# Recurrent-memory attention block with gradients: second buffers for exponentials and turned O in the forward stage, and the work around them rearranged

## The chip, the cores and the metric

The kernel runs on one core of one Trainium2 chip. The metric is the device time of one execution in microseconds (us). The engines of the core are called as in the profile: PE is TensorE (the matrix unit; PEld is its loading of weights), DVE is VectorE, ACT is ScalarE, POOL is GpSimd and SP is SyncE, which here only issues transfers (DMAs). "SPq" in a row is the transfer queue that SP feeds.

## The reference

A transformer block with conditioning, forward and backward: the kernel returns the output and the gradients of eleven inputs. The forward part is:

```
mod = (silu(c) @ w_mod)  split into  sa, ca, ga, sb, cb, gb      # 6 rows of 512
h = layernorm(x) * (1 + ca) + sa
x = x + ga * A(h)
h = layernorm(x) * (1 + cb) + sb
x = x + gb * ((sigmoid(h @ w_gate) * (h @ w_up)) @ w_down)       # w_gate: 512 x 1792

A(h):  mem = mem0                               # 8 rows of 512
  for s in range(64):                           # 2048 tokens, 32 a segment
    h_s = concat(mem, h[32 tokens of s])        # 40 rows
    q, k, v = h_s Wq, h_s Wk, h_s Wv            # 32 heads of 128
    p = softmax(mask(q k^T / sqrt(128)))        # causal; the 8 memory columns are always seen
    o = (p v) Wo
    mem = o[:8];  out_s = o[8:]
```

The eight memory rows that leave a segment enter the next one, so the 64 segments are one chain in the forward part and again, the other way, in the backward part. x has 2048 rows of 512.

## The kernel before

The work is a row of stages, each a method of one class: setup and the first LayerNorm, the forward attention (`phase2`, about 45 to 957 us of the profiled span), the gated block (`phase3`, to about 1600 us), the backward attention and the last products. The change lies in `phase2` and in what it loads and computes ahead for `phase3`.

`phase2` runs a loop over the 64 segments `s`; `s4 = s % 4` is the place of a segment in a row tile, since four segments of 32 tokens fill the 128 rows in which LayerNorm works. The 32 heads are laid out in `G = 11` groups of three. One segment goes like this:

- `proj` and `v_chunk`: q, k and v of the segment from its turned rows `hT` (products into `pass_ps`, copies into the row buffers `RA` and `Vst`, two each). `rows_out` stores the q and k rows on SP's queue (L604, L605). `turns` turns q and k by heads into `XT`.
- `st_exp`: the scores, three pieces into `st_ps`, and ScalarE's exponentials into `ET` (L869). There is one `ET`.
- SP transposes `Vst` into `VTr` (L1007) and `ET` into `Pst` (L1015), both by DMA; there is one buffer of each. They, O and turned O are kept in memory for the backward part. `norm`, put off to the beginning of the next segment, lets GpSimd scale `Pst` by the reciprocal sums `rden` (L1091) and SP store `VTr` and `Pst` (L1093, L1094).
- `den` and `pv`: sums and p v from `ET` into `or_ps` (L873 is the matmul of the sums). `ost` scales them into `Ost`, one buffer (VectorE for the first and the third piece at L917, ScalarE for the second); TensorE turns `Ost` in `tps` (L885) and the copies (L63 on VectorE, L61 on ScalarE, which are the two lines of the common helper `evac`) make `OT`, turned O. There is one `OT`. SP stores `Ost` to OSR (L1044) and `OT` (L1061).
- `outproj`: the product with Wo into `at_ps` (`pair_mm`, L223, 64 small matmuls). `split_pair` (L227 to L233) splits the result into `at_hi` (ScalarE, L230) and `at_lo` (VectorE, L232), `sum_pair` adds the two through TensorE (`at_ft`, L242), and ScalarE copies the first eight columns into the next segment's `hT`: that closes the chain. `store_rows` sends the other rows to AOA (L345).

Four other kinds of work are laid between these steps:

- LayerNorm for the row tiles ahead: `p1(j, k)` runs step `k` of tile `j` (0 load at L396, 1 statistics at L400, 2 scale, 3 shift, 4 turn). With `P1_AHEAD = 2` the statistics come in segments with `s4 = 2`, the scale in `s4 = 3`, the shift in `s4 = 0`, the turn in `s4 = 1`.
- The eight last rows of the four segments of a tile are projected together for q and k (`b_pieces`): products into `RB`, stored at L609 and L612 in `s4 = 1` and 2, turned into the tail columns `b_cols` of k and q (pool `p2bt`, two buffers). `tails_in` (GpSimd copies) puts the eight columns of the next segment into `XT`; `v_tails` (GpSimd DMAs) does this for v.
- `TailRows` collects the eight last columns of `OT` of each of the four segments (`collect`) in one tile, and turns them into rows with products laid between the steps of the next four segments (`chunk`, `split`).
- The first row tile of the gated block is begun in the last segments (`first_tile_steps`): loads of x, of attention output rows (AOA) and of the gradient rows, broadcasts of the conditioning rows 2 to 5, then residual, LayerNorm and turn.

Program order on each engine is the order in which the code calls these (`self.pin(i0)` holds it as written); the tile pools add the waits that a buffer's reuse needs. All transfers named above but GpSimd's go through SP's one queue in its program order. The beginning of `phase3` is touched as far as SP loads its row tiles behind this stage: VectorE's GLU chain starts at L1206, TensorE turns w_down at L1182.

Of the kernel before, what the change touches and what calls it, by code (L numbers as in the profile page):

```python
# [40 lines left out]
class K:  # L41
# [336 lines left out]
    def phase1_setup(self, ctx, psum_tile_fn):  # L378
# [55 lines left out]

        return p1_tile
# [9 lines left out]
    def phase2(self):  # L445
# [15 lines left out]
        with ExitStack() as ctx:  # L461
# [29 lines left out]
            ET = ptiles("ET", 1)[0]  # L491
            Vsts = ptiles("Vst", 2)
            Ost = ptiles("Ost", 1)[0]
            OT = ptiles("OT", 1)[0]
# [55 lines left out]
            btp = ctx.enter_context(tc.tile_pool(name="p2bt", bufs=2))  # L550
# [67 lines left out]
            def b_pieces(t):  # L618
# [14 lines left out]
                def turn_b(x):  # L633
                    bt[x] = btp.tile([128, 8, 128], BF16, name="b_cols" + x)
# [4 lines left out]
                    def f():  # L639
                        for hf in range(2):  # L640
# [79 lines left out]
            def first_tile_steps():  # L720
# [5 lines left out]
                bc = {2: self.sa_bc[:], 4: self.ca1_bc[:]}  # L726
                x1, sm = self.first_x1, self.first_st

                def load():
# [3 lines left out]
                    nc.sync.dma_start(dout, io["grad_out"].rearrange("o s d -> (o s) d")[0:128, :])  # L733
                    nc.gpsimd.memset(sm[:, 10:11], -0.5)

                def load_mod():
                    for i, x in ((3, "k"), (5, "q")):
                        bc[i] = f32(btails[NT - 2][x][:].rearrange("p i x -> p (i x)"))
                    for i in (2, 5, 4, 3):
                        nc.sync.dma_start(bc[i], self.MODROW[:, i * D:(i + 1) * D].rearrange("o d -> (o d)").partition_broadcast(128))  # L740

                def gates():
                    nc.vector.tensor_tensor(db, dout, bc[5], op=ALU.mult)
# [21 lines left out]
                def mods():  # L765
                    for i in (2, 5, 3):
                        nc.gpsimd.tensor_copy(self.bcs[i], bc[i])
                    nc.gpsimd.tensor_scalar_add(self.bcs[4], bc[4], 1.0)
# [8 lines left out]
                return load, load_mod, gates, add, stats, scale, rows, mods, turn  # L777
# [11 lines left out]
            tail = TailRows(self, sb2, psp, psp, 1, "ao", rows_b, (8, 16, 8), ptag="p")  # L789
# [34 lines left out]
            for s in range(NS):  # L824
# [13 lines left out]
                QT, KT, Vst = XT["q"], XT["k"], Vsts[s % 2]  # L838
# [164 lines left out]
                if 0 < s < NS - 1:  # L1003
                    v_chunk(s, 2)
                    v_tails(s + 1)
                if s < NS - 1:
# [39 lines left out]
                evac_turned()  # L1046
                for k in {0: (1, 2), 1: (3,)}.get(s, ()):
                    p1(P1_AHEAD, k)
                if s4 in (0, 2) and s > 0:
                    p1(s // nseg_t + P1_AHEAD + (s4 > 0), {2: 1, 0: 3}[s4])  # L1050
                if NS - 4 <= s < NS - 1:
                    first_tile[s - NS + 4]()
                elif s == NS - 1:
                    first_tile[6]()
                if s + 1 < NS:
                    tails_in("kq", s + 1)
                parts = self.split_pair(sb2, at_ps, "at")
                if s4 == 3:
                    p1(s // nseg_t + P1_AHEAD + 1, 2)
                tail.collect(s4, [OT])  # L1060
# [22 lines left out]
                if s4 == 0:  # L1083
                    tail.chunk()
                tail.split()
# [1213 lines left out]
class TailRows:  # L2299
# [3 lines left out]
    def __init__(self, k, pool, psp, psb, n, name, dram_b, npieces=4, home=None, ptag="b"):  # L2303
        self.k, self.pool, self.psp, self.psb, self.n, self.name = k, pool, psp, psb, n, name
        self.dram_b, self.npieces, self.home, self.ptag = dram_b, npieces, home, ptag
        self.cur = None
# [3 lines left out]
    def collect(self, s4, tiles):  # L2310
        nc, cfg = self.k.nc, self.k.cfg
        if self.cur is None:
            self.cur = [self.pool.tile([128, 33, 32], BF16, name=f"{self.name}_tail{i}") for i in range(self.n)]
# [145 lines left out]
```

## Time and profile before

| | us |
|---|---|
| three runs | 2984.21, 2986.32, 2985.37; median 2985.37 |
| profiled execution | 2986.66, of which span 2984.7 |
| forward stage, about | 45 to 957 |
| PE busy over the span | 2916.5 |
| PE busy in 45 to 250, 250 to 500, 500 to 750, 750 to 957 us | 197.23, 247.67, 245.22, 197.33 |
| mean granted clock of TensorE | 0.996 |

The page of the profile gives busy times, the chain and the groups of instructions over the whole span; the views that the trace answers give the same for a stretch. A row of the waits names the waiting engine, the tile that it wanted to write or read, what it waited for, the sum in us, how many waits and the mean of one. A row of the timeline gives the start in us, the duration, the engine, the line, the operation with its tiles, and in brackets the idle time before it with what ended it. A row of a tile gives the fewest, median and most ns of an instruction and where the first and the last began. The shares of busy time over the whole span mix stages with different limits; those of a stretch do not.

### The profile page before, as it was taken

The page shows a single profiled execution, that of the slowest core. Times are in us where ns is not written, and L with a number is a line of the kernel's source. Part 1 is how long each engine was busy: PE and PEld are TensorE (multiplying, and loading weights), DVE is VectorE, ACT ScalarE, POOL GpSimd, SP SyncE. Part 2 cuts the span into 40 slices and gives each one's busy share as a digit, 9 for nine tenths or more (in the row PEclk, how much of TensorE's full clock was granted, in tenths as well). Part 3 has the DMA queues.
Part 4 walks back from the last instruction along what each step waited for, and adds up shares of the span by engine and source line. Part 5 has one row for each costly group of instructions (what it writes and reads, how often), then busy time and mean ns, then how long its engine had stood idle before and what let it go on. Part 6 is the DMA issues. An engine that isn't in the chain of part 4 may idle for free.

```text
span 2984.7 us, 105439 instructions
## 1 busy us (share of the span) xinstructions
PE 2916.5 (98%) x43816; PEld 1817.4 (61%) x43816; DVE 1622.8 (54%) x3680; ACT 1348.8 (45%) x3244; POOL 1235.0 (41%) x2485
## 2 busy tenths in 40 slices
PE   6999999999998999999999999999999999999999
PEld 3666666666665544445677777777777754445555
DVE  5665666665554788833365566656566632850011
ACT  3666666666665533312355555555555520110011
POOL 2555555554555222221244444444444422762111
PEclk9999999999999999999999999999999999999999
DMA  9988999888889899998699999999999997886565
GB/s 309 225 215 220 215 214 225 215 218 207 217 218 270 210 229 233 229 282 280 202 249 234 266 249 250 255 253 250 252 250 252 247 280 249 253 262 190 160 216 171
DMA packets 837922, 703.01 MB, mean 236 GB/s; under 512 B 537682, under 2 KB 709890, under 8 KB 836548
## 3 DMA queue, kind: packets, MB, share of 16 engines
q1 hardware_dynamic: 711828, 485.29, 66.2%
q0 software_dynamic: 54512, 148.63, 15.7%
q10 hardware_dynamic: 71104, 62.34, 6.5%
q8 instruction: 345, 5.65, 0.8%
q14 instruction: 133, 1.09, 0.1%
HBM read 294.99 MB, written 276.35 MB: 191 GB/s over the span
## 4 chain that ended last, share of the span: by engine, by line
PE 69%; DMA 2%; ACT 1%; DVE 1%; issue 1%; SPq 0%; POOL 0%; DVEq 0%; ACTq 0%; POOLq 0%
PE gps L2240 14%; PE dh_ps L215 8%; PE pass_ps L257 7%; PE g_ps L1863 5%; PE gps5o L2255 4%; PE dhq_ps L223 4%; PE mm L1344 3%; PE dh_tps L215 3%; PE gps L1523 3%; PE mm L1304 2%; PE mm L1319 2%; PE tps L1780 2%; PE mm L1277 1%; PE mm L1273 1%; PE gps L1422 1%; PE dp_ps L1840 1%
## 5 line engine op out<-in xcount | busy, mean ns | idle before, releaser
L2240 PE MATMUL gps<-rows,hrows 128*128 128x512 bf16 (+2 forms) x2160 | 415.5, 355 | 0.0
L2240 PEld LDWEIGHTS <-hrows 128*128 128x128 bf16 x2160 | 211.1, 98 | 204.6 <-issue 0.9
L1091 POOL TENSOR_TENSOR Pst<-Pst,rden 120x1408 bf16<-120x1408 bf16 x63 | 159.8, 2537 | 265.2 <-issue 190.5
L63 DVE CAST ot<-gps 128x512 bf16<-128x512 f32 (+3 forms) x76 | 48.1, 634 | 308.7 <-PE gps L2240 222.3
L1908 POOL COPY dOst<-RAd 96x512 bf16<-96x512 bf16 x128 | 75.5, 613 | 296.7 <-DVE RAd L63 296.5
L61 ACT ACTIVATE ot<-gps 128x512 bf16<-128x512 f32 (+3 forms) x75 | 41.2, 550 | 346.8 <-PE gps L2240 214.2
L673 PE MATMUL pass_ps<-Wv,hT 128*32 128x512 bf16 (+2 forms) x2304 | 186.2, 357 | 0.0
L2244 POOL DMA_DIRECT2D out_dram<-ot x104 | 78.7, 757 | 254.7 <-DVE ot L63 132.0
L257 PEld LDWEIGHTS <-hT 128*32 128x32 bf16 x4096 | 114.5, 97 | 97.8 <-POOL hT L559 4.1
L63 DVE CAST Vst<-pass_ps 96x512 bf16<-96x512 f32 x128 | 87.3, 682 | 106.7 <-ACT RBv L61 103.2
L223 PE MATMUL at_ps<-Wo,OT 128*32 128x256 bf16 x4096 | 129.4, 278 | 6.4 <-DVE OT L63 3.6
L215 PE MATMUL dh_ps<-WvT,dVT 128*32 128x512 bf16 x2048 | 133.5, 381 | 1.4 <-DVE RBd L63 0.2
L673 PE MATMUL pass_ps<-Wv,hb 128*32 128x512 bf16 (+2 forms) x636 | 127.2, 346 | 1.1 <-DMA Wv<-in_A_Wv_dram 1.1
L257 PE MATMUL pass_ps<-Wk,hT 128*32 128x512 bf16 x2048 | 122.3, 380 | 2.1 <-DVE mv L402 1.1
L257 PE MATMUL pass_ps<-WoT,dyT 128*32 128x256 bf16 (+1 forms) x3072 | 122.6, 308 | 0.9 <-ACT dyT L1989 0.9
L223 PE MATMUL dhq_ps<-WqT,dQT 128*32 128x256 bf16 x4096 | 123.2, 273 | 0.1
L257 PE MATMUL pass_ps<-Wq,hT 128*32 128x512 bf16 x2048 | 122.7, 379 | 0.0
L215 PE MATMUL dh_ps<-WkT,dKT 128*32 128x512 bf16 x2048 | 122.3, 380 | 0.0
L2255 PE MATMUL gps5o<-WoT,rows 128*128 128x512 bf16 x560 | 121.0, 379 | 0.0
L223 PEld LDWEIGHTS <-dQT 128*32 128x32 bf16 x4096 | 109.7, 97 | 16.2 <-issue 0.4
L317 DVE TENSOR_TENSOR dST<-dh_ps,dST 128x512 bf16<-128x512 f32 x64 | 44.3, 692 | 130.1 <-ACT dST L316 130.1
L223 PEld LDWEIGHTS <-OT 128*32 128x32 bf16 x4096 | 99.3, 98 | 25.7 <-ACT OT L61 6.4
(475 smaller groups left out, 7051.8 us busy)
## 6 DMA issues: line engine op xcount, KB each, us to landing
OSR<-Ost SPq DMA_DIRECT2D x64, 352.0 KB
OT<-OT SPq DMA_DIRECT2D x64, 352.0 KB
PS<-Pst SPq DMA_DIRECT2D x64, 352.0 KB
Pst_l<-PS SPq DMA_DIRECT2D x64, 352.0 KB
OT_l<-OT SPq DMA_DIRECT2D x64, 352.0 KB
DVR<-rows_x POOLq DMA_DIRECT2D x64, 352.0 KB, 6.4
DKR<-rows_x POOLq DMA_DIRECT2D x64, 352.0 KB, 5.8
DQR<-rows_x POOLq DMA_DIRECT2D x64, 352.0 KB, 3.3
```

The lines of the kernel that those rows point to most:

```text
L63: return nc.vector.tensor_copy(out, in_)
L215: self.nc.tensor.matmul(ps[32 * j:32 * j + 32, :], lhsT=lhsT, rhs=w, start=(n < 4), stop=(n >= total - 4), tile_position=(0, 32 * j))
L223: nc.tensor.matmul(ps[32 * j:32 * j + 32, :], lhsT=x[k], rhs=w[k][:, 256 * d:256 * d + 256], start=(n == 0), stop=(n == total - 1), tile_p ...
L257: self.nc.tensor.matmul(ps[32 * j:32 * j + 32, :], lhsT=lhs(c), rhs=rhs, start=(c == 0), stop=(c == DC - 1), tile_position=(0, 32 * j))
L673: nc.tensor.matmul(ps[32 * j:32 * j + 32, o * E:(o + n) * E], lhsT=lhsT, rhs=wc[:, 3 * a + hl:3 * (a + n - 1) + hl + 1:3, :], start=(c == ...
L1091: nc.gpsimd.tensor_tensor(Pst[0:120, :, :], Pst[0:120, :, :], rden[:, :].unsqueeze(2).to_broadcast([120, G, 128]), op=ALU.mult)
L1344: nc.tensor.matmul(hp[:], lhsT=xT[:, fc, :], rhs=wT[:, fc, :], start=(n == 0), stop=(n == 2 * FC - 1))
L1523: nc.tensor.matmul(ps[:], lhsT=h2r[:, j, c * 128:(c + 1) * 128], rhs=xr[:, j, :], start=(j == 0), stop=(j == NT - 1))
L1863: nc.tensor.matmul(ps[:, j, 0:w], lhsT=lh[:, g * GW:(g + 1) * GW], rhs=rh[:, g * GW:g * GW + w], start=True, stop=True)
L2240: nc.tensor.matmul(ps[:, 0:ng * E], lhsT=hrows[:, tp_, c * 128:(c + 1) * 128], rhs=rows[:, tp_, 0:ng * E], start=(tp_ == 0), stop=(tp_ == ...
L2244: (nc.sync if i == len(todo) - 1 else nc.gpsimd).dma_start(outw[c * 128:(c + 1) * 128, h0:h0 + 3 * (ng - 1) + 1:3, :], ot[:, 0:ng * E].rea ...
L2255: nc.tensor.matmul(pss[gg][:], lhsT=rows[:, t, gg * E:(gg + 1) * E], rhs=dyrows[:, t, :], start=(n == 0), stop=(n == NTP - 1))
```

## The change

There are two buffers of `ET` and two of `OT`, chosen by the parity of the segment. Room for them comes from the pool of the tail columns `b_cols` and the tile of `TailRows`, which go from two buffers to one. With one buffer the collection of the segments with `s4 = 0` moves behind the third piece of products (`chunk`), the tail columns are taken at the copies and not at the turn, and `tails_in` for the next segment moves ahead, behind `v_tails`, in segments other than the first and those with `s4 = 3`. `split_pair` stands ahead of the LayerNorm steps of the segment, where the statistics and the shift stood ahead of it. The loads for the first tile of the gated block, six at segment 60 and four at 61, are spread over segments 54 to 56 and 59 to 61 and issued between the stores of `Ost` and `OT`; the one of row 5 comes in two halves into other tiles, and what uses it works in halves. The other stages are the same.

```
--- before.py
+++ after.py
@@ -432,6 +432,8 @@
 
             return load, stats, scale, shift, turn
 
+        self.xh_tile = lambda: p1w.tile([128, D], F32, name="xh", bufs=1)[:]
+        self.hx_tile = lambda: p1w.tile([128, DC, 128], BF16, name="hx", bufs=3)[:]
         return p1_tile
 
     def rstd_from_var(self, out, var, pool, n):
@@ -488,10 +490,10 @@
             nc.gpsimd.dma_start(self.AOA[0, 0:M, :], io["A_mem0"].rearrange("o m d -> (o m) d"))
             XT = {x: ptiles(x + "T", 1, w=cfg.XW)[0] for x in "qk"}
             VTr = pt.tile([128, G, 128], BF16, name="VTr")
-            ET = ptiles("ET", 1)[0]
+            ETs = ptiles("ET", 2)
             Vsts = ptiles("Vst", 2)
             Ost = ptiles("Ost", 1)[0]
-            OT = ptiles("OT", 1)[0]
+            OTs = ptiles("OT", 2)
             RAs = [{x: ptiles(f"RA{i}" + x, 1, w=9 * 128)[0] for x in "kq"} for i in range(2)]
             RB = {x: ptiles("RB" + x, 1, w=9 * 128)[0] for x in "kq"}
             RBv = ptiles("RBv", 2)
@@ -547,7 +549,7 @@
                 nc.sync.dma_start(Wv[:, :, :], io["A_Wv"].rearrange("(c p) h e -> p c (h e)", p=128))
                 place["q"] = self.load_heads(stage(1), Wq, io["A_Wq"], 2)
                 place["k"]()
-            btp = ctx.enter_context(tc.tile_pool(name="p2bt", bufs=2))
+            btp = ctx.enter_context(tc.tile_pool(name="p2bt", bufs=1))
             sb2 = ctx.enter_context(tc.tile_pool(name="p2s2", bufs=2))
 
             hts = {}
@@ -631,12 +633,12 @@
                             store()
 
                 def turn_b(x):
-                    bt[x] = btp.tile([128, 8, 128], BF16, name="b_cols" + x)
                     tp = psp.tile([128, 8, 128], BF16, name="turn_ps", tag="p")
                     for i in range(8):
                         nc.tensor.transpose(tp[:, i, :], RBt[x][:, i * 128:(i + 1) * 128], self.ident[:, :])
 
                     def f():
+                        bt[x] = btp.tile([128, 8, 128], BF16, name="b_cols" + x)
                         for hf in range(2):
                             self.evac(("act", "dve")[hf], bt[x][:, 4 * hf:4 * hf + 4, :], tp[:, 4 * hf:4 * hf + 4, :])
 
@@ -724,23 +726,41 @@
                 dout, db = RB["q"][:, 0:D], RB["q"][:, D:2 * D]
                 xhf = f32(RBv[NT % 2][:, 0:2 * D])
                 bc = {2: self.sa_bc[:], 4: self.ca1_bc[:]}
+                bc5 = []
                 x1, sm = self.first_x1, self.first_st
 
-                def load():
+                def bc_load(i, dst, a=0, n=D):
+                    row = self.MODROW[:, i * D + a:i * D + a + n]
+                    nc.sync.dma_start(dst, row.rearrange("o d -> (o d)").partition_broadcast(128))
+
+                def bc_2():
+                    bc_load(2, bc[2])
+
+                def bc_4():
+                    bc_load(4, bc[4])
+
+                def bc_3():
+                    bc[3] = self.xh_tile()
+                    bc_load(3, bc[3])
+
+                def x_rows():
                     nc.sync.dma_start(x0, io["A_x"].rearrange("o s d -> (o s) d")[0:128, :])
                     for i in range(4):
                         nc.sync.dma_start(ar[32 * i:32 * i + 32, :], self.AOA[i + 1, M:M + T, :])
+                    nc.gpsimd.memset(sm[:, 10:11], -0.5)
+
+                def dout_rows():
                     nc.sync.dma_start(dout, io["grad_out"].rearrange("o s d -> (o s) d")[0:128, :])
-                    nc.gpsimd.memset(sm[:, 10:11], -0.5)
-
-                def load_mod():
-                    for i, x in ((3, "k"), (5, "q")):
-                        bc[i] = f32(btails[NT - 2][x][:].rearrange("p i x -> p (i x)"))
-                    for i in (2, 5, 4, 3):
-                        nc.sync.dma_start(bc[i], self.MODROW[:, i * D:(i + 1) * D].rearrange("o d -> (o d)").partition_broadcast(128))
+
+                def bc_5():
+                    for i in range(2):
+                        bc5.append(f32(self.hx_tile().rearrange("p c x -> p (c x)")))
+                        bc_load(5, bc5[i], D // 2 * i, D // 2)
 
                 def gates():
-                    nc.vector.tensor_tensor(db, dout, bc[5], op=ALU.mult)
+                    for i in range(2):
+                        sl = slice(D // 2 * i, D // 2 * i + D // 2)
+                        nc.vector.tensor_tensor(db[:, sl], dout[:, sl], bc5[i], op=ALU.mult)
                     nc.gpsimd.dma_start(self.DBROWS[0:128, :], db)
                     nc.vector.tensor_tensor(x1[:], ar, bc[2], op=ALU.mult)
 
@@ -763,8 +783,10 @@
                     nc.gpsimd.dma_start(self.H2ROWS[0:128, :], h2)
 
                 def mods():
-                    for i in (2, 5, 3):
+                    for i in (2, 3):
                         nc.gpsimd.tensor_copy(self.bcs[i], bc[i])
+                    for i in range(2):
+                        nc.gpsimd.tensor_copy(self.bcs[5][:, D // 2 * i:D // 2 * i + D // 2], bc5[i])
                     nc.gpsimd.tensor_scalar_add(self.bcs[4], bc[4], 1.0)
 
                 def turn():
@@ -774,7 +796,8 @@
                         nc.tensor.transpose(tp[:, i, :], src[:, (i % DC) * 128:(i % DC) * 128 + 128], self.ident[:, :])
                     nc.scalar.activation(self.first_hdT, tp[:], AF.Copy)
 
-                return load, load_mod, gates, add, stats, scale, rows, mods, turn
+                loads = {NS - 10: bc_2, NS - 9: bc_4, NS - 8: bc_3, NS - 5: x_rows, NS - 4: dout_rows, NS - 3: bc_5}
+                return loads, None, gates, add, stats, scale, rows, mods, turn
 
             first_tile = first_tile_steps()
             norms = []
@@ -786,7 +809,7 @@
                     nc.gpsimd.dma_start(self.AOA[4 * b + i + 1, 32:32 + M, :].rearrange("r (c x) -> (r c) x", x=128),
                                         rb[32 * i:32 * i + 32, :])
 
-            tail = TailRows(self, sb2, psp, psp, 1, "ao", rows_b, (8, 16, 8), ptag="p")
+            tail = TailRows(self, sb2, psp, psp, 1, "ao", rows_b, (8, 16, 8), ptag="p", bufs=1)
 
             masked = {}
 
@@ -835,7 +858,7 @@
                     slots.update(first_piece)
                 hT = get_ht(s)
                 hT_next = get_ht(s + 1) if s + 1 < NS else None
-                QT, KT, Vst = XT["q"], XT["k"], Vsts[s % 2]
+                QT, KT, Vst, ET, OT = XT["q"], XT["k"], Vsts[s % 2], ETs[s % 2], OTs[s % 2]
                 RA = RAs[s % 2]
                 rden = sb2.tile([120, G], F32, name="rden")
 
@@ -1003,6 +1026,8 @@
                 if 0 < s < NS - 1:
                     v_chunk(s, 2)
                     v_tails(s + 1)
+                    if s4 < 3:
+                        tails_in("kq", s + 1)
                 if s < NS - 1:
                     nc.sync.dma_start(VTr[:], Vst[:, :], transpose=True)
                 or2 = ps_f32("or_ps")
@@ -1044,20 +1069,21 @@
                 nc.sync.dma_start(self.OSR[s], gl3(Ost))
                 at_ps = outproj()
                 evac_turned()
+                if s in first_tile[0]:
+                    first_tile[0][s]()
+                elif s == NS - 2:
+                    first_tile[2]()
+                elif s == NS - 1:
+                    first_tile[6]()
+                if s + 1 < NS and (s == 0 or s4 == 3):
+                    tails_in("kq", s + 1)
+                parts = self.split_pair(sb2, at_ps, "at")
                 for k in {0: (1, 2), 1: (3,)}.get(s, ()):
                     p1(P1_AHEAD, k)
-                if s4 in (0, 2) and s > 0:
-                    p1(s // nseg_t + P1_AHEAD + (s4 > 0), {2: 1, 0: 3}[s4])
-                if NS - 4 <= s < NS - 1:
-                    first_tile[s - NS + 4]()
-                elif s == NS - 1:
-                    first_tile[6]()
-                if s + 1 < NS:
-                    tails_in("kq", s + 1)
-                parts = self.split_pair(sb2, at_ps, "at")
-                if s4 == 3:
-                    p1(s // nseg_t + P1_AHEAD + 1, 2)
-                tail.collect(s4, [OT])
+                if s4 != 1 and s > 0:
+                    p1(s // nseg_t + P1_AHEAD + (s4 > 0), {2: 1, 3: 2, 0: 3}[s4])
+                if s4:
+                    tail.collect(s4, [OT])
                 nc.sync.dma_start(self.OT[s], gl3(OT))
                 fill(s4, "f1")
                 if s == NS - 1:
@@ -1082,6 +1108,7 @@
                     mod_r.append(products)
                 if s4 == 0:
                     tail.chunk()
+                    tail.collect(s4, [OT])
                 tail.split()
                 self.store_rows(psp, sb2, ft, self.AOA[s + 1, 0:32, :], "at", "p")
                 if s4 == nseg_t - 1:
@@ -2300,17 +2327,18 @@
 
 
 
-    def __init__(self, k, pool, psp, psb, n, name, dram_b, npieces=4, home=None, ptag="b"):
+    def __init__(self, k, pool, psp, psb, n, name, dram_b, npieces=4, home=None, ptag="b", bufs=2):
         self.k, self.pool, self.psp, self.psb, self.n, self.name = k, pool, psp, psb, n, name
         self.dram_b, self.npieces, self.home, self.ptag = dram_b, npieces, home, ptag
-        self.cur = None
+        self.cur, self.bufs = None, bufs
         self.pieces = []
         self.whole = None
 
     def collect(self, s4, tiles):
         nc, cfg = self.k.nc, self.k.cfg
         if self.cur is None:
-            self.cur = [self.pool.tile([128, 33, 32], BF16, name=f"{self.name}_tail{i}") for i in range(self.n)]
+            self.cur = [self.pool.tile([128, 33, 32], BF16, name=f"{self.name}_tail{i}", bufs=self.bufs)
+                        for i in range(self.n)]
         for t, b in zip(tiles, self.cur):
             src = t[:, 0:11 * 128].rearrange("p (g x) -> p g x", x=128)[:, :, 96:120]
             src = src.rearrange("p g (a r) -> p g a r", r=8)
```

More of the change, by code (lines that the diff above doesn't have):

```diff
@@ L775, in turn @@
                     nc.scalar.activation(self.first_hdT, tp[:], AF.Copy)
[L777 removed]
+                loads = {NS - 10: bc_2, NS - 9: bc_4, NS - 8: bc_3, NS - 5: x_rows, NS - 4: dout_rows, NS - 3: bc_5}
+                return loads, None, gates, add, stats, scale, rows, mods, turn
             first_tile = first_tile_steps()
```

82 lines of the change are left out of this document (52 added, 30 removed).

## The prediction

> **What bounds the kernel now.** I read the page first, then the waits of TensorE (PE) in the forward stage, then who else waited there, then the transfer queue of SyncE (SP) in order of time.
>
> ```profile
> span 2984.7 us, 105439 instructions
> PE 2916.5 (98%) x43816; PEld 1817.4 (61%) x43816; DVE 1622.8 (54%) x3680; ACT 1348.8 (45%) x3244; POOL 1235.0 (41%) x2485
> ```
>
> TensorE is idle for 68 us of the span; only what it waits for can be won. The forward stage runs from about 45 to 957 us. Its waits of TensorE, in 55 to 945 us:
>
> ```profile
> PE or_ps L873 <- ACT ET L869: 5.8, 12, 2.0
> PE at_ft L242 <- DVE at_lo L232: 4.7, 16, 0.3
> PE at_ps L223 <- DVE OT L63: 3.4, 2, 2.9
> PE tps L885 <- DVE Ost L917: 3.2, 16, 0.4
> ```
>
> The first and third are ends of chains that start at transfers, as the waits of ScalarE (ACT) in the same stretch show:
>
> ```profile
> ACT ET L869 <- DMA Pst<-ET: 8.8, 5, 2.9
> ACT OT L61 <- DMA OT<-OT: 2.7, 1, 2.7
> ```
>
> So both single buffers do stop the chain. But what makes the transfers late? This is ET's own answer in 60 to 940 us: 62 transposes of segments 0 to 61, and the exponentials of segments 1 to 62 (three each).
>
> ```profile
> L869 ACT ACTIVATE ET<-st_ps x186: 477/564/572, 64.6 to 934.3; 128x480 bf16<-128x480 f32 x124, 128x360 bf16<-128x360 f32 x62
> L1015 SPq DMA_TRANSPOSE Pst<-ET x62: 1277/1800/3324, 60.9 to 927.2; - x62
> ```
>
> From the first transpose issue to the last are 927.2 - 60.9 = 866.3 us, 866.3/61 = 14.20 us a segment. TensorE is quicker: the hT copies that close the segments lie 13.96, 14.02, 14.39 and 14.12 us apart for s4 = 0 to 3 wherever nothing stops it, and 13.96 in s4 = 2 where no LayerNorm is left (segments 54 and 58). And SP is never idle for TensorE's sake. One lap of it, then the wait behind which all its idle time lies (100 to 900 us):
>
> ```profile
> 722.76 0.38 SPq L1094 DMA_DIRECT2D PS<-Pst  x1
> ...
> 727.55 1.40 SPq L1007 DMA_TRANSPOSE VTr<-Vst  x1
> 729.05 1.50 SPq L1015 DMA_TRANSPOSE Pst<-ET  x1
> 730.64 0.80 SPq L1044 DMA_DIRECT2D OSR<-Ost  x1
> ...
> 737.20 0.32 SPq L1094 DMA_DIRECT2D PS<-Pst  x1
> ```
>
> ```profile
> SPq L1094 <- POOL Pst L1091: 74.1, 30, 2.7
> ```
>
> The lap closes on itself: Pst's transpose lands 4 to 6 us after issue, GpSimd (POOL) scales it (2.54), SP stores it, sends the K and Q rows, transposes V, transposes ET again into the one Pst. In the s4 = 1 and 2 segments SP issues without a gap instead (708.48 to 722.76 us, 14.3 us). Nothing in it waits for TensorE. Until segment 40 SP only falls behind (Pst issued 2.8 us after the exponentials of segment 20, 9.0 after those of 47); then the exponentials wait for it.
>
> **The change, part by part.** The sum is made against the profiled execution (2986.66 us, span 2984.7, so 1.96 around it), which is 1.29 above the median of 2985.37; I carry the difference over to the median.
>
> *Second ET.* It takes away 8.8 us of ScalarE's waits. What is late next is Ost, still single: its store is issued right behind ET's transpose (729.05 + 1.50, then 730.64) on the same queue. In the trace's packets that store ends 0.1 to 0.3 us after the scaling of Pst begins (which begins about 0.65 after the transpose's own last packet), so it is visible at 0.9 by the same delay. Ost is first written 1.75 us after the exponentials begin (309.07 and 307.32 in segment 18). The new room is 1.75 - 0.9 = 0.85 us of lag, once, for SP's laps stay as long as they are. Bounds: 0 (Ost as early as ET) to the 8.8.
>
> *Second OT.* OT's store is later still. In segment 52 the turned O starts 0.55 us late (796.25), which goes. In segment 62 OT's store stood behind four broadcast loads:
>
> ```profile
> 939.42 0.41 DVE L63 COPY OT<-tps 128x480 bf16<-128x480 bf16 x1 [2.91 <-DMA OT<-OT]
> 939.88 3.25 PE L223 MATMUL at_ps<-Wo,OT 128*32 128x256 bf16 x64 [2.87 <-DVE OT L63]
> 956.00 1.93 PE L223 MATMUL at_ps<-Wo,OT 128*32 128x256 bf16 x64 [0.19 <-DVE OT L63]
> ```
>
> The idle 2.87 us and 3.25 - 1.93 = 1.32 of slowed matmuls go (the granted clock is 0.5 for 3.4 us behind that idle time): -4.2. It is the end of the stage, so no lap of SP can take it back there. Behind the 2.05 us idle of segment 1 the clock is also 0.5 (at_ps takes 3.60), behind the 1.47 of segment 48 it is not. The Trainium skill (TensorE: Matmul & The Clock Gate, Part 1) has the clock halved after an idle window of about 3.4 us; by that rule the sum would count 2.87 here and end 1.3 later. The trace disagrees (2.05 and 2.87 were enough), and I go by it.
>
> *LayerNorm behind the split.* In the 13 s4 = 2 segments that have it (2 to 50) statistics stood before at_lo:
>
> ```profile
> 312.71 0.68 DVE L400 BATCH_NORM_STATS2 st<-x 128x6 f32<-128x512 bf16 x1
> 312.86 0.38 ACT L230 ACTIVATE at_hi<-at_ps 128x256 bf16<-128x256 f32 x1 [0.53 <-PE at_ps L223]
> 313.71 0.41 DVE L232 TENSOR_TENSOR at_lo<-at_ps,at_hi 128x256 bf16<-128x256 f32 x1
> 314.18 0.27 PE L242 MATMUL at_ft<-foldsel,at_lo 128*128 128x32 bf16 x4 [0.31 <-DVE at_lo L232]
> ```
>
> at_lo can start at 313.3: 14.39 - 13.96 = 0.43 each, 13 x 0.43 = 5.6 us of TensorE. Behind it 0.68 + 0.18 + 0.15 of VectorE push the next cast 0.7 later, into 0.75 us of idle VectorE before the K cast at 315.92: nothing. But 14.39 only falls towards 14.02, further below the 14.20 of SP: the 5.6 turn into lag, and from about segment 20 into waits for Ost. I take 0, ends 0 and -5.6. The same for the 4.4 of segment 1 (2.05 idle, the rest slow clock): lag that segments 2 to 4 hand back.
>
> *Tail columns.* Per segment six GpSimd copies (2 x 0.64 us) move ahead of the AOA store (0.57), behind the scaling of Pst (2.54) and the V tails (1.57). GpSimd is 59% idle and nobody waits for AOA rows: nothing. But with one buffer of tail columns ScalarE's write of b_colsk, 3.0 us after the exponentials of s4 = 2, waits for the k copies, 2.54 + 1.57 + 0.65 + 0.1 = 4.9 us after the scaling began; behind it stand at_hi and hT. With the scaling 0.85 us into the exponentials (1.4 long) that is 1.35 late. TensorE that waits lets SP catch up, so it is paid from lag: 0, end +1.35 once. Collecting s4 = 0's columns behind the third piece delays only hT of the segment after next: 0.
>
> *Loads spread.* Six issues at segment 60 (914.94 to 918.53) and four at 61 (1 MB, 2.9 us of SP) become: three broadcasts at 54 to 56, five rows at 59, one at 60, two halves at 61, all between Ost's and OT's stores. In s4 = 3 and 0 SP idles 2.5 to 5 us behind OT's store for the scaling, which covers them; in 54 (0.4 to 1.3 us) nothing does. Pst of 61 comes about 1 us earlier: that lets segment 62 follow, -0.2. Ends -1 and +1.3.
>
> *Start.* Two more memsets (0.65 each), both ahead of the gate products: 1.3 us late, covered by TensorE's waits for Wv (1.1), Wq (1.4) and Wo (1.8): 0, end +1.3. Gates in halves: +0.1 of VectorE under 1.93 us of at_ps.
>
> *Leaving the stage.* TensorE comes out 0.85 + 0.55 + 0.2 + 4.2 = 5.8 us earlier, SP about 2 to 4. The row tiles of the next stage are SP's loads, in contention with three weights of 1.8 MB:
>
> ```profile
> 970.57 0.69 DVE L1206 TENSOR_TENSOR t<-Wv 128x512 f32<-128x512 bf16 x1 [4.67 <-DMA Wv<-AOA]
> ...
> 977.36 0.55 PE L1182 MATMUL tp<-ident,Wv 128*128 128x128 bf16 x7 [1.52 <-DVE w_downT L63]
> ```
>
> VectorE waits there, and TensorE behind it. If the rows move by 3.5, that 1.52 grows by 2.3: +2.3. Ends: 0 (the weights start 5.8 earlier too, and the transfers move with them) and 2.3 + 1.7, half a 3.4 us stretch at half clock, = +4.
>
> Sum: -5.8 + 2.3 = -3.5: 2985.37 - 3.5 = **2981.9 us**. Own range of this case: -5.8 + 0 - 1 to -5.8 + 4 + 1.35, 2978.6 to 2984.9.
>
> **Rivals.**
> *A, the queue yields.* If SP's lap were shortened by an earlier TensorE, all would arrive: ET 5.4 (the excess of segments 40 to 52 over the undisturbed lengths), segment 1 4.4, LayerNorm 5.6, OT 4.2 = 19.6, less 2.3 to 4 at the exit: about 2968.5; with laps 1% shorter, worked through segment by segment, -8.8 up to segment 62 instead of -1.6: 2974.7. For it: laps differ (53.7 us for the four segments from 52, 59.9 from 44). Against: they do not depend on how far SP is behind. The Trainium skill (Trainium Kernel Development and Optimization, Best Practices) says to double-buffer to overlap transfers with compute; by that rule this case is the outcome, and no run here shows it yet.
> *B, the exit takes it all.* Rows move by nothing, TensorE idles 1.5 + 5.8 and pays 1.7 of slow clock: 2985.37 - 5.8 + 5.8 + 1.7 = 2987. For it: SP has no slack; against: the weights move.
> *C, slower.* The issue of the two transposes lengthens (L1007, L1015: 1.28 to 3.32 us, median 1.80), because TensorE now always runs at the limit of the lag and the V tails of GpSimd fall between them. Each 0.1 us a lap costs 6.1 us; from 0.16 us (6 + 3.5 over 61) it is slower by over 0.2%; at 0.2, 2985.4 - 3.5 + 12.2 = 2994. Against: lap and lag are unrelated above.
>
> **Numbers.** Forecast 0.53, A 0.27, B 0.12, C 0.08. 0.2% (6 us) is about what a measurement of this kernel can tell. Below 2979.4: A and 0.08 of the forecast, 0.35; above 2991.3: C, 0.08; between: 0.57. The range reaches into A and B: 2970 to 2988.
>
> **What would show it.** Right: no ET <- DMA waits of ScalarE but VectorE's Ost <- DMA OSR; s4 = 2 segments of 13.96 where nothing stops them; Pst's transposes still 14.2 us apart; no OT wait in 62; a longer L1182 wait at the exit. Wrong: laps below 14.1, no Ost waits, or b_colsk waiting for GpSimd.

## The result and the profile after

The changed kernel takes 2978.58 us (median of 9) against 2985.37 for the kernel before (median of 9): ratio 0.9973, interval 0.9963 to 0.9984, so 4.8 to 11 us faster. One of the nine executions of the changed kernel took 3669.26 us at a granted clock of 0.753; the ratio is that of the others. A second comparison on another chip gave 0.9964 (0.9951 to 0.9978). The forecast was 2981.9; the time lies between it and rival A.

The page of the changed kernel:

```profile
span 2974.4 us, 105326 instructions
PE 2905.7 (98%) x43742; PEld 1816.9 (61%) x43816; DVE 1620.3 (54%) x3683; ACT 1348.0 (45%) x3244; POOL 1233.2 (41%) x2486
```

By the sums TensorE is idle for 68.7 us, as before, but here they say little: 74 of its 43816 matmul records are missing (x43742), and what is missing looks idle. Where the time went is read from the stage's own marks. First the waits of TensorE in 55 to 945 us, then those of ScalarE and of VectorE (us in total, times, longest):

```profile
PE tps L908 <- DVE Ost L940: 7.8, 22, 1.1
...
PE at_ft L242 <- DVE at_lo L232: 0.9, 5, 0.2
PE or_ps L896 <- ACT ET L892: 0.2, 1, 0.2
PE at_ps L223 <- DVE OT L63: 0.2, 1, 0.2
```

```profile
ACT Ost L937 <- DMA OSR<-Ost: 3.1, 5, 1.1
...
ACT b_colsk L61 <- POOL kT L65: 1.8, 3, 0.9
```

```profile
DVE Ost L940 <- DMA OSR<-Ost: 4.0, 5, 1.3
```

The waits for ET and OT are gone (5.8 and 3.4 us of TensorE before), those for at_lo fell from 4.7 to 0.9, and Ost took ET's place: 7.8 in place of 3.2. The one buffer of tail columns costs three waits of up to 0.9.

The tile ET of the changed kernel (fewest, median and most ns, first and last start), then its tile hT, then the tile hT of the kernel before:

```profile
L1040 SPq DMA_TRANSPOSE Pst<-ET x63: 1386/1867/3216, 60.3 to 929.1; - x63
```

```profile
L1099 ACT ACTIVATE hT<-at_ft x63: 197/197/198, 56.4 to 930.8; 128x32 bf16<-128x32 f32 x63
```

```profile
L1073 ACT ACTIVATE hT<-at_ft x63: 197/198/198, 55.0 to 944.4; 128x32 bf16<-128x32 f32 x63
```

The last hT comes at 930.8 in place of 944.4: 13.6 us, where the forecast had 5.8. And the lap of SP, which the forecast took as fixed, is 868.8/62 = 14.01 us in place of 14.20. The lengths of TensorE between hT copies, where nothing stops it, are 13.97, 14.02, 13.96 and 14.00 us for s4 = 0 to 3 (before 13.96, 14.02, 14.39, 14.12). The s4 = 2 segment of the forecast, 18, again in order of time:

```profile
310.44 0.38 ACT L230 ACTIVATE at_hi<-at_ps 128x256 bf16<-128x256 f32 x1 [0.53 <-PE at_ps L223]
310.86 0.42 DVE L232 TENSOR_TENSOR at_lo<-at_ps,at_hi 128x256 bf16<-128x256 f32 x1 [0.49 <-ACT at_hi L230]
...
311.20 0.68 DVE L400 BATCH_NORM_STATS2 st<-x 128x6 f32<-128x512 bf16 x1
...
311.34 0.27 PE L242 MATMUL at_ft<-foldsel,at_lo 128*128 128x32 bf16 x4
```

at_lo follows at_hi at once and the statistics stand behind it: 311.34 - 310.44 = 0.90 from at_hi to the product, 1.32 before. And segment 62, where the copy into OT waited 2.91 us before, so that the product with Wo (L223) began 2.87 us late and ran slowly:

```profile
927.13 0.40 DVE L63 COPY OT<-tps 128x480 bf16<-128x480 bf16 x1
...
927.65 1.94 PE L223 MATMUL at_ps<-Wo,OT 128*32 128x256 bf16 x64
```

The product has no wait and full speed (1.94 in place of 3.25). Behind the stage, TensorE's largest stops in the changed kernel:

```profile
948.99 1.91 PE L215 MATMUL ao_tps<-Wo,ao_tail 128*32 128x512 bf16 x32 [2.54 <-DVE Pst L929]
...
965.23 0.55 PE L1209 MATMUL tp<-ident,Wv 128*128 128x128 bf16 x7 [2.15 <-DVE w_downT L63]
```

The second was 1.52 before, the first 1.26: 1.91 us of the gain is given back here. The forecast's reason for it, that SP comes out later than TensorE does, is not shown: in the three profiles that the experiments give of each kernel, one of them with a longer start, the two stops together are 2.78, 2.52 and 4.59 us before and 4.69, 4.48 and 3.40 after.

### The profile page after: what moved, and what is told of

Same layout as the page of the kernel before. It is cut to its first block, busy times and chain, and to the rows that moved or that the text cites. A ratio compares the mean times of both kernels' runs of the same rounds, so it can differ in the third digit from the quotient of the medians.

```text
span 2974.4 us, 105326 instructions
## 1 busy us (share of the span) xinstructions
PE 2905.7 (98%) x43742; PEld 1816.9 (61%) x43816; DVE 1620.3 (54%) x3683; ACT 1348.0 (45%) x3244; POOL 1233.2 (41%) x2486
## 4 chain that ended last, share of the span: by engine, by line
PE 89%; DMA 5%; DVE 2%; issue 2%; ACT 1%; SPq 1%; POOL 1%; DVEq 0%; POOLq 0%; ACTq 0%
PE gps L2267 14%; PE pass_ps L257 14%; PE dh_ps L215 8%; PE g_ps L1890 5%; PE pass_ps L675 5%; PE gps5o L2282 4%; PE dhq_ps L223 4%; PE at_ps L223 4%; PE mm L1371 3%; PE gps L1550 3%; PE dh_tps L215 3%; PE turn_ps L880 2%; PE mm L1331 2%; PE mm L1346 2%; PE tps L1807 2%
## 5 line engine op out<-in xcount | busy, mean ns | idle before, releaser
L223 PE MATMUL at_ps<-Wo,OT 128*32 128x256 bf16 x4096 | 127.8, 276 | 1.2 <-ACT OT L61 1.0
L223 PE MATMUL dhq_ps<-WqT,dQT 128*32 128x256 bf16 x4096 | 122.9, 273 | 0.0
L223 PEld LDWEIGHTS <-dQT 128*32 128x32 bf16 x4096 | 109.8, 97 | 15.7
L1877 DVE SCALAR_TENSOR_TENSOR dS<-dp_ps,Pst_l 128x480 bf16<-128x480 f32 (+1 forms) x192 | 106.3, 610 | 10.0 <-PE dp_ps L1875 4.1
```

Source lines behind the costliest of these rows:

```text
L223: nc.tensor.matmul(ps[32 * j:32 * j + 32, :], lhsT=x[k], rhs=w[k][:, 256 * d:256 * d + 256], start=(n == 0), stop=(n == total - 1), tile_p ...
L1877: nc.vector.scalar_tensor_tensor(out=part3(dS, pi)[:, :, 0:120], in0=ps[:, 0:n, 0:120], scalar=cfg.scale, in1=part3(Pst, pi)[:, :, 0:120], ...
```

## The experiments

The kernels of a group ran on one chip, beside the kernel before. Laps are given from here on as the distance between the starts of Pst's transposes of segments 1 and 61, over 60, from each run's trace; on that measure the first profiles have 14.23 (before) and 14.07 (after). A lap is that of the one profiled execution, which can lie some us off its kernel's median.

While reading the two traces I found a candidate for the shorter lap, and tested it first. In the kernel before, GpSimd began to scale Pst 0.6 to 0.75 us behind the last packet of ET's transpose in most segments, and up to 2.8 us behind it in some. Segment 35 is a late one, segment 36 is not (GpSimd's scalings in order of time; the last packets ended at 558.45 and 574.07; what the brackets name is inferred, and what the scaling needs is the transpose):

```profile
560.82 2.54 POOL L1091 TENSOR_TENSOR Pst<-Pst,rden 120x1408 bf16<-120x1408 bf16 x1 [3.84 <-DMA OT<-OT]
...
574.70 2.54 POOL L1091 TENSOR_TENSOR Pst<-Pst,rden 120x1408 bf16<-120x1408 bf16 x1 [5.87 <-issue]
```

The transfers of 558 to 559.5 us show what lay on the DMA engines in the late one (queue: packets, MB, share):

```profile
q1 hardware_dynamic: 372, 0.42, 79.9%
q8 instruction: 1, 0.02, 3.9%
```

One 16 KB packet of instructions, 0.94 us long, started with the end of the transpose. In 574 to 575 us there is none.

**The same two kernels again, and both with the fetches shifted.** The shift:

```
+                pad_ps = psp.tile([128, 128], BF16, name="pad_ps", tag="p")
+                for i in range(64):
+                    nc.tensor.transpose(pad_ps[:], self.ident[:, :], self.ident[:, :])
                 m_ps = psp.tile([120, 120], F32, name="mask_ps", tag="p")
```

> The kernel before, unchanged, for a second profile. In its first profile the scaling of Pst on GpSimd began about 0.65 us behind the last packet of ET's transpose in 49 of 61 segments, and 1.0 to 2.8 us behind it in 12; in 11 of those 12 a 16 KB packet of an instruction fetch lay on one DMA engine around that moment. The mean delay was 0.97 us, in the changed kernel 0.76 (4 or 5 late segments), and the laps of SP were 14.23 and 14.03 us. Theory F (fetches): lap = 14.0 + 1.5 x the share of late segments; which segments are late hangs on where the fetches of TensorE's program fall against SP's queue, so in this profile the lap follows the count by that formula, whatever the count is. Rival Y (the queue yields to an earlier TensorE): the lap is 14.2 again, and the count says nothing of it.

> The changed kernel, unchanged, for a second profile and a tighter time. Theory F: lap = 14.0 + 1.5 x the share of late segments; time 2975 to 2982 us, with the profile at the count's place in it (each late segment up to 1.5 us of lap). Rival Y: lap 14.0 again, also if 10 segments are late.

> The kernel before with 64 idle transposes more at the head of TensorE's program (128 instructions, half of a 16 KB fetch, while TensorE waits for the mask). They cost up to 1 us at the start and shift every later fetch by half its size against the work. Theory F: the set of late segments is another one; if it falls from 12 to 5 the laps become 14.1 and the time 2978 to 2981 us, if it stays near 12 the time is 2984 to 2988. Rival Y: 14.2 us a lap and 2985 to 2987 us, whatever the count.

> The same 64 transposes in the changed kernel. Theory F: with 10 to 12 late segments in place of 4 the laps become 14.2 us and the time 2983 to 2987; with 4 again 2977 to 2981. Rival Y: 14.0 us a lap and 2977 to 2981, whatever the count.

| | ratio to before (interval) | lap | delays over 1 us, of 60 | last hT |
|---|---|---|---|---|
| before | 1 | 14.23 | 13 | 944.4 |
| before, again | one run: 2992.6 us | 14.32 | 5 | 951.0 |
| before, shifted | 1.001 (0.9998 to 1.0022) | 14.20 | 13 | 941.1 |
| after | 0.9973 (0.9963 to 0.9984) | 14.07 | 5 | 930.8 |
| after, again | 0.9964 (0.9951 to 0.9978) | 14.04 | 5 | 929.6 |
| after, shifted | 0.9988 (0.9976 to 0.9999) | 14.17 | 5 | 936.2 |

Theory F falls as the explanation of the lap. The kernel before made 5 late segments at 14.32 us a lap, more than its first profile with 13. The delay itself is real: over the eleven profiles of this study in which SP stores Pst, 61 scalings began more than 1.7 us late, and at all 61 a 16 KB fetch lay on a DMA engine between 0.1 us before the end of the transpose and 0.5 us behind it; it lay there also in 73 segments that were not late, and without a fetch the mean delay is 0.66 to 0.74 us. But 2 to 10 such events a profile do not order the laps.

The table shows something else as well. The changed kernel with a head of 64 transposes in idle time has 0.9988 in place of 0.9964 (the intervals just touch) and laps of 14.17. Differences of 0.1 us a lap, 6 us, can come with nothing changed in the loop; single parts of that size are read with care below.

**LayerNorm alone, and everything but LayerNorm.**

```
 before, LayerNorm behind the split:
-                for k in {0: (1, 2), 1: (3,)}.get(s, ()):
-                    p1(P1_AHEAD, k)
-                if s4 in (0, 2) and s > 0:
-                    p1(s // nseg_t + P1_AHEAD + (s4 > 0), {2: 1, 0: 3}[s4])
...
                 parts = self.split_pair(sb2, at_ps, "at")
-                if s4 == 3:
-                    p1(s // nseg_t + P1_AHEAD + 1, 2)
+                for k in {0: (1, 2), 1: (3,)}.get(s, ()):
+                    p1(P1_AHEAD, k)
+                if s4 != 1 and s > 0:
+                    p1(s // nseg_t + P1_AHEAD + (s4 > 0), {2: 1, 3: 2, 0: 3}[s4])
 after, LayerNorm ahead again: the same lines the other way
```

> The kernel before with the LayerNorm steps behind the split and nothing else. TensorE's own length falls by 0.43 us in the 13 segments of s4 = 2 and by 0.12 in those of s4 = 3, 7.4 us in all. Theory Q (mine in the prediction: SP's laps have a length of their own): the laps stay at 14.2 to 14.3 us and ScalarE's waits for Pst<-ET grow from 9 to about 15 us; time 0 to 2 us below the kernel before. Theory Y (what TensorE saves arrives): laps near 14.1, waits as before, time 6 to 8 us below.

> The changed kernel with the LayerNorm steps ahead of the split again; buffers, tail columns and loads stay changed. Theory Q: time within 2 us of the changed kernel (10 us below the kernel before), the waits for Ost about 2 us instead of 7.8. Theory Y: 6 to 8 us above the changed kernel (2 to 4 us below the kernel before), waits for Ost as large as in the changed kernel.

LayerNorm alone gave 0.9987 (0.9978 to 0.9997), 3.9 us; everything but LayerNorm 0.9985 (0.9973 to 0.9997), 4.5 us. Together 8.4, which is what the change gives (8.1 and 10.8 by its two ratios). The first lies between theory Q's 0 to 2 and theory Y's 6 to 8, and its interval, 0.9 to 6.6 us, reaches into both. The 7.4 of the expectation was itself wrong: s4 = 3 segments stayed at 14.12 us here and were 14.00 with LayerNorm back, so those 0.12 belong to the rest of the change, and LayerNorm is 5.6. Of 5.6 about 4 arrived. The waits are nearer to theory Y. Theory Q wanted more of them; ScalarE's waits for ET in the kernel with LayerNorm alone are fewer than before (8.8):

```profile
ACT ET L869 <- DMA Pst<-ET: 5.9, 5, 2.4
```

Its transposes of ET lie (932.4 - 60.3)/62 = 14.07 us apart, on the measure of before (14.20):

```profile
L1015 SPq DMA_TRANSPOSE Pst<-ET x63: 1378/1910/3047, 60.3 to 932.4; - x63
```

With LayerNorm back, theory Q wanted about 2 us of waits for Ost and a time 10 us below the kernel before, theory Y 7.8 us and 2 to 4; the time is 4.5 below (0.9 to 8.1), and TensorE waits:

```profile
PE tps L908 <- DVE Ost L940: 6.4, 22, 1.0
```

The laps are 14.08 with LayerNorm alone and 14.23 with LayerNorm back. With that, the profiles with the statistics ahead of at_lo have 14.23, 14.32, 14.20 and 14.23, and those with them behind 14.07, 14.04, 14.17 and 14.08. But the profile with LayerNorm back is of the slowest of its twelve executions, 2988.26 us where the median is 2979.78; if those 8.5 us lay in the laps, they would be 0.14 of each.

**Does SP follow TensorE?** In the changed kernel, the first sums twice:

```
                 den(0, or2)
+                den(0, or2)
                 den(1, or2)
```

> The changed kernel with the first sums (den of the first piece, four small matmuls into the same place) made twice: 0.25 us more for TensorE in each of 64 segments, 16 us in all, nothing for SP. Undisturbed segments become 14.24 us on the mean in place of 13.99. Theory Q: SP's laps stay at 14.04 to 14.17, TensorE is the slower one and the waits for Ost go; the time rises by 62 x (14.24 - 14.10) = 8 to 10 us. Theory Y: laps follow TensorE one to one and the waits stay; the time rises by 15 to 16 us.

Undisturbed segments became 14.05 to 14.11 us, 14.08 on the mean and not 14.24. The matmuls of the sums in segment 18 show why, first in the changed kernel, then here:

```profile
305.88 0.37 PE L896 MATMUL or_ps<-ones,ET 128*128 128x1 bf16 x8
```

```profile
306.41 0.45 PE L896 MATMUL or_ps<-ones,ET 128*128 128x1 bf16 x12
```

They overlap: eight take 0.37 us from the first start to the last end, twelve 0.45. The 0.25 of the expectation is what four take when they stand alone (at 939.86 in the changed kernel). So the step is 0.09 a segment, 5.4 us in 62, a third of what was meant. The time was 0.9970 (0.9959 to 0.9982), 2 us above the 0.9964 of the changed kernel in another group, with intervals that hold 0 and 5.4 alike. The waits:

```profile
PE tps L908 <- DVE Ost L940: 5.1, 21, 0.5
```

7.8 and 7.5 in the two profiles of the changed kernel, and 12.6 in the shifted one, became 5.1, which leans to theory Q. The laps are 14.09, within the 14.04 to 14.17 of those three. But laps that follow TensorE would be only 0.09 longer than those, 14.13 to 14.26, and this profile is of an execution 4.4 us below its kernel's median, which is up to 0.07 a lap. So the experiment does not separate the theories: theory Y, and with it rival A's mechanism, is neither shown nor refuted.

**The second buffers.** One ET with two OT, and two Ost in place of two OT:

```
-            ETs = ptiles("ET", 2)
+            ETs = 2 * ptiles("ET", 1)
 the other kernel:
-            Ost = ptiles("Ost", 1)[0]
-            OTs = ptiles("OT", 2)
+            Osts = ptiles("Ost", 2)
+            OTs = 2 * ptiles("OT", 1)
 ... (and Ost is Osts[s % 2] in segment s)
```

> The changed kernel with one ET; OT keeps two buffers. By the prediction the second ET moves the limit from ET to Ost, 0.85 us of room once: ScalarE's waits for Pst<-ET come back with about 8 us in place of the 7.8 for Ost, and the time stays within 2 us of the changed kernel (8 to 11 below the kernel before). Rival: the second ET is worth the whole wait, 8 to 9 us, and the time is near the kernel before.

> The changed kernel with two buffers of Ost in place of two of OT (room in the memory is for one of them). If Ost is what stops TensorE now, VectorE's and ScalarE's waits for OSR<-Ost (6 us) go and TensorE's waits for Ost fall from 7.8 to about 3.5 (those of 0.2 to 0.4 us that are there in any case); OT's store, 1 to 3 us later than Ost's with OT written 3.8 us later, limits next. Theory Q (SP's laps have their own length): about 2 us of room once, time 1 to 3 us below the changed kernel. Theory Y: 4 to 6 us below it.

With one ET the ratio is 0.9982 (0.9969 to 0.9995). The waits came back as expected:

```profile
ACT ET L892 <- DMA Pst<-ET: 7.7, 7, 2.5
...
ACT Ost L937 <- DMA OSR<-Ost: 1.6, 1, 1.6
```

In the same group the kernel with two Ost had 0.9964, so the second ET would be worth some 5 us; the intervals overlap, and its lap (14.11) is of an execution 8.5 us below the median of its kernel (2976.27 and 2984.82). Between the 2 and the 8 that were set against each other it is not settled.

Two Ost (0.9964, interval 0.9949 to 0.9978) brought what the forecast's chain says: no wait for OSR<-Ost is left, TensorE's waits for Ost fell to the short ones that are always there, and OT is next:

```profile
PE tps L908 <- DVE Ost L940: 3.8, 18, 0.4
...
PE at_ps L223 <- DVE OT L63: 2.4, 5, 1.1
```

The time is that of the changed kernel (0.9964 in another group). A second Ost in place of the second OT moves the wait and gives nothing that can be seen; SP's lap stays: 14.04.

**SP freed.** One line, in the kernel before, in the changed one, and in the one with LayerNorm alone:

```
                     nc.sync.dma_start(self.VT[s], VTr[:])
-                    nc.sync.dma_start(self.PS[s], Pst[:])
+                    nc.gpsimd.dma_start(self.PS[s], Pst[:])
```

> The kernel before with one line changed: the scaled Pst is stored from GpSimd's queue and not from SP's, so SP no longer waits for the scaling (1.77 us of idle time a lap, and 0.4 of issue). Theory: SP's lap would be 14.2 - 2.1 = 12.1 us, less than TensorE's 14.10, so SP runs up to TensorE, the waits of ScalarE for Pst<-ET (8.8 us) and of the first OT wait of segment 52 go, and nothing else does: 5 to 8 us below the kernel before (segment 62's wait behind four broadcasts shrinks too). Rival (the lap is bound by the DMA engines, 0.9 busy, and not by SP's idle time): laps stay at 14.0 or more, waits stay, time within 2 us of before.

> The same line in the changed kernel. Theory: the waits for Ost (7.8 us) go and the stage ends 6 to 8 us earlier than in the changed kernel; the next stage's row tiles come earlier with SP, so most of it arrives: 15 to 17 us below the kernel before. Rival: no difference to the changed kernel.

> The kernel before with the LayerNorm steps behind the split and Pst stored from GpSimd's queue: single buffers everywhere, loads of the next stage as before, SP free of the wait for the scaling. If the second buffers only cover SP's lateness, they are worth little here: 5 to 6 us (LayerNorm) below the one-line kernel of before, so 11 to 13 us below the kernel before, and the changed kernel with the same line is 3 to 5 us better still. If they are worth more by themselves, the difference to that one is above 6 us.

| | ratio to before (interval) | us below before |
|---|---|---|
| before + line | 0.9977 (0.9966 to 0.9988) | 6.9 |
| LayerNorm + line | 0.9957 (0.9942 to 0.9972) | 12.9 |
| after + line | 0.9945 (0.9931 to 0.9958) | 16.4 |

SP's largest wait in 100 to 900 us is now that of the V transpose and no longer the store of Pst (73.6 us in the changed kernel). This is the changed kernel with the line (the first row names ScalarE's last work before the issue ended; what the transpose reads is Vst, which VectorE, ScalarE and transfers of GpSimd fill):

```profile
SPq L1032 <- ACT Ost L937: 68.0, 32, 2.6
```

```profile
PE tps L908 <- DVE Ost L940: 4.8, 19, 1.2
```

```profile
L1040 SPq DMA_TRANSPOSE Pst<-ET x63: 1319/1678/3787, 60.2 to 921.8; - x63
```

```profile
L1099 ACT ACTIVATE hT<-at_ft x63: 197/197/198, 54.9 to 925.1; 128x32 bf16<-128x32 f32 x63
```

SP follows TensorE here: over segments 1 to 61 its transposes lie 13.95 us apart and the hT copies 14.02. The line is worth 6.9 us in the kernel before and, by 0.9945 against 0.9964 to 0.9973, 6 to 8 in the changed one. In the kernel before it takes ScalarE's waits for the one ET from 8.8 to 3.1 us, and segment 62 takes 13.95 us with one OT and with the loads where they were: with SP on time these cost little. With SP free, LayerNorm gives 12.9 - 6.9 = 6.0, near its 5.6, and the rest of the change 16.4 - 12.9 = 3.5; both are differences between groups, uncertain by 5 to 6 us either way, so the second is not clear of zero. The changed kernel with the line (2967.0 us where the kernel before had 2984.0) beats both.

The Trainium skill (DMA: Bandwidth & Descriptors, Issuing engines are not separate DMA queues) says that issuing from several engines saves only the time to initiate a transfer, usually small. Here the issue was 0.4 us a lap; what counted was the wait for the scaling that stood at the head of SP's queue, 73.6 us of its idle time, with everything else behind it.

## Why the prediction was right, and where it was not

The time (2978.58) lies in the range of 2970 to 2988 and just outside the edge of the likeliest case's own range (2978.6). The sum had -3.5 us; measured are -6.8 by the medians, -8.1 by the ratio and -10.8 by the ratio of the second comparison. That the time lies in the range is owed to its reach into rival A more than to the sum. Of the three signs of being wrong that the prediction names, two were seen: laps below 14.1, and b_colsk waiting for GpSimd. The waits for Ost came as forecast. Step by step:

- *SP never waits for TensorE.* Nearly right as a reading of the trace: between its instructions SP stands still for 118 us in 100 to 900 us of the kernel before, of which 97 lie ahead of the store of Pst and 14 ahead of the V transposes, 0.25 each.
- *Second ET: 0.85 us of lag, Ost is next.* The chain is right in each link: the ET waits went, the waits for OSR came, and with two Ost the waits for OT. The size is not settled (about 5 us by the kernel with one ET, within the scatter).
- *Second OT and the loads of segment 62: -4.2.* Right in these two profiles: the segment takes 13.95 us in place of 18.21. In the other two profiles with the old stage it took 20.07 and 14.26, so 3.6 on the mean of the three.
- *LayerNorm: -5.6 for TensorE, 0 in time.* This is the step that failed. TensorE's part is right to the hundredth (14.39 to 13.96). But "SP's laps stay as long as they are" is not: they became 14.07. The sum took 0 between its ends of 0 and -5.6; LayerNorm alone gave 3.9 us (0.9 to 6.6), and about 6.0 with SP free.
- *s4 = 3 segments.* Not foreseen: 14.12 to 14.00, 15 x 0.12 = 1.8 us, with the parts of the change other than LayerNorm.
- *Tail columns, end +1.35.* ScalarE waits three times for the k copies, at most 0.9. Right in kind; what it cost in time was not measured by itself.
- *Start: 0.* The first hT came at 55.0, 56.2 and 56.0 in the kernels with the old stage and at 56.4, 56.5 and 54.7 in those with the new one. The two memsets are not to be seen in it.
- *Leaving the stage: +2.3.* Right as a sum, within a scatter of up to 5 us. From the last hT to the end of the span are 2040.3, 2039.7 and 2044.6 us in three profiles before and 2043.6, 2041.7 and 2045.3 in three after: +2.0. The wait ahead of w_down's turns (L1182, after the change L1209), which was to grow by 2.3, has 1.52, 1.25 and 3.04 before and 2.15, 3.21 and 2.14 after: 0.6 on the mean.

In the mean of those three and three profiles the stage ends 13.3 us earlier (945.5 to 932.2). The lap gives 61 x (14.25 - 14.09) = 9.6 of it, the end of the stage 3.6 (segment 62 took 18.2, 20.1 and 14.3 us before, 13.95 after). The forecast had 5.8 for the two together. 13.3 - 2.0 = 11.3 is above the 6.8 and 10.5 of the medians; three profiles a side carry a lap's scatter of 0.05 us, 3 us each.

Rival A gave the right direction for the failed step; whether its reason is right is open, as said above. Rivals B and C did not happen. By the Best Practices rule of the Trainium skill (Trainium Kernel Development and Optimization) the second buffers should have overlapped the transfers; in these runs they moved the wait from ET to Ost, and two Ost in place of two OT moved it to OT. Only together with the line that takes the wait out of SP's queue, which needs no buffer, did the gain come near to that of case A (16.4 us; 16.9).

Why the laps are shorter with the statistics behind at_lo stays open, and the difference is less sure than it looks: 14.24 on the mean of the four profiles with the statistics ahead, 14.09 in the seven behind that have SP store Pst. The four profiled executions lie 2.6 us above their kernels' medians on the mean, the seven 3.5 below; if all of that lay in the laps, it would make 0.10 of the 0.16. It need not lie there: the profile with LayerNorm and the line is 7.2 us above its median with a lap of 14.02, and 2053.0 us lie behind its last hT, where the others have 2037.5 to 2045.6.

The share of late scalings as a whole does not explain the difference. TensorE's own pace where nothing stops it, 14.12 us in the four on the mean and 14.01 in the seven, would give 0.11 if the laps followed it; that they do is not shown. The difference is largest in the laps of s4 = 3 (13.40 us in the four, 13.03 in the seven), 0.30 of it between the transpose's last packet and the scaling; of those laps 14 of 60 were late by over 1 us ahead and 4 of 105 behind. That a fetch meets that one landing less often when the segment before is 0.43 us shorter would fit, but this was only argued, not tried.

## What to carry to other kernels

When a wait for a buffer hangs on an in-order transfer queue that is itself late, a second buffer moves the wait to the next buffer; look for the instruction at which the queue sits idle (here the store of Pst, 74 of 800 us) and take that wait to another queue. A lap length read from one profile is a sample: the same kernel gave 14.23 and 14.32 us, which over 61 laps is 6 us, as much as the effect under study. Before a queue's pace is called fixed, a second profile is worth its time, and the time of each profiled execution belongs beside the median of its kernel.

## What the runs showed of the hardware

- Instruction fetches lie on the DMA engines beside the data, as the rows of segment 35 show: one 16 KB packet took 0.94 us there. All 61 scalings that began more than 1.7 us behind the last packet of their transpose had such a packet at its end, and so had 73 that were not late; the usual delay is 0.7 us, the late ones are mostly 2.1 to 2.4. The fetch as the cause is inferred from this meeting; no run is without fetches. The Trainium skill (Runtime: NRT & Kernel Launch, Instruction fetch mechanics) has the fetch in 16 KiB blocks over a DMA queue and its cost mostly hidden; the size of the blocks agrees.
- 64 idle transposes at the head of TensorE's program, in time in which it waited, went with 3 us more in the kernel before (0.9998 to 1.0022, so not clear of zero) and about 7 in the changed one (0.9988 against 0.9964).
- Matmuls with one column overlap: four alone took 0.25 us, eight in a row 0.37, twelve 0.45. Four more made a segment 0.09 us longer.
